# FFT filter and squared-ReLU FFN: a quarter of stage A moved, casts moved from VectorE to GpSimd

## The chip, the cores and the metric

The kernel runs on one core of a Trainium2 chip. Five engines work side by side: TensorE (PE, matmuls; its weight loads have a row of their own, PEld), VectorE (DVE), ScalarE (ACT), GpSimd (POOL) and SyncE (SP, which here issues nearly all DMAs). The metric is the device time of one execution in microseconds (us); lower is better.

## The reference

The input x has 8 batches of 3008 rows by 256 columns. Each batch is filtered along its rows in the frequency domain, and the result goes through a feed-forward network (FFN) with a squared ReLU.

```python
def _attn_ref(x, filt_r, filt_i):            # x (8, 3008, 256), filters (1505, 256)
    X = np.fft.rfft(x, axis=1)
    F = (filt_r + 1j * filt_i)[None, :, :]
    Y = X * F
    return np.fft.irfft(Y, n=x.shape[1], axis=1).astype(np.float32)

def _moe_ref(x, w_in, w_out):                # x (24064, 256), w_in (256, 2048), w_out (2048, 256)
    h = np.maximum(x @ w_in, 0.0)
    return (h * h @ w_out).astype(np.float32)
```

## The kernel before

The Fourier transform of 3008 = 64 x 47 points is done as matmuls with constant matrices, in stages, for one batch at a time:

- Stage A (`unit_a`, 16 units of a batch, four of them filling one tile u): matmuls into PSUM, and a cast of the 96x512 result into u in SBUF. In batches 2 to 7 the input is a tile of x cast to 16 bits (`cast_x`, 94x2048, four tiles a batch); batch 1 reads other tiles, `xw16`, and needs two matmuls a unit. Each full u is written to a DRAM buffer dU (`write_u`).
- `read_u` brings dU back in another layout as ut. Stage B (`unit_b`, 12 units) is two matmuls and, on DVE, the product with the filter, read from PSUM into prod, then two copies of half a tile across partitions (yf), then (`unit_s`) an add. `unit_p` takes yf through two more matmuls, ACT evacuates them into ze, and ze goes to DRAM (dZ).
- `read_z` brings dZ back as zt. Stage Y (`unit_y`, 16 units) is four small matmuls, evacuated by ACT (even units) or DVE (odd units) into yt, the FFN's input.

The FFN goes over 47 groups of 512 tokens. A group has eight slots. `ffn_g1` computes an eighth of the hidden layer, four matmuls into psH; ACT applies the ReLU into h; DVE squares h in place (`ffn_sq`); `ffn_g2` computes a half of one 128-token block of the group before (eight matmuls, psO). The loop at lines 728 to 739 writes the order out by hand: in slot s comes g1 of this group, the FFT work planned for place 0, g2 of the group before, the FFT work of place 1, the output, the square. Each engine works through its own instructions in that order, so an instruction that waits holds all behind it on its engine.

`fft_plan(b)` (line 610) says in which slot which unit of batch b runs. Slots are counted from a first slot of the batch: 0 for batch 1, and 40, 88, 136, 184, 232, 280 for batches 2 to 7, all multiples of eight. In batch 1 the plan also holds the rest of batch 0's stage Y and the four casts of W_out (`cast_wout`, 128x1024 each, on DVE). In batch 1 three quarters of stage A are done ahead of the loop by `chunk_a`; the plan has the last four units, 12 to 15, in slots 8 and 9. Stage B takes slots 14 to 31 in batch 1 and 19 to 37 later. The x of the next batch is loaded and cast in the same plan: two loads ahead of stage B's middle, and two that wait for the casts of the first two, since the pool of x in 32 bits has two buffers.

Tiles come from pools with a fixed number of buffers: a new tile waits until the last readers of the one that had its buffer are done. The ones that matter: psF (two buffers, shared by stages A, B, P and Y in turn), psH (two), `p_u` (u, three), `p_x16` (x in 16 bits, and `xw16`, four), `p_x32` (two), `p_h2` (h, and in the beginning W_out in 32 bits, two). In group 0 there is no g2 yet, so its slots are about half as long as the others.

Of the kernel before, what the change touches and what calls it, by code (L numbers as in the profile page):

```python
# [9 lines left out]
F16 = mybir.dt.float16  # L10
# [100 lines left out]
def kernel(  # L111
# [9 lines left out]
    nc = tc.nc  # L121
    B, S, D = x.shape
# [18 lines left out]
    p_x16 = ctx.enter_context(tc.tile_pool(name="p_x16", bufs=4))  # L141
    p_u = ctx.enter_context(tc.tile_pool(name="p_u", bufs=3))
# [14 lines left out]
    def psF(name):  # L157
        return pps.tile([128, 512], F32, tag="psF", name=name, bufs=2)
# [176 lines left out]

    x16s, us, uts, prods, zes, zts, yts = {}, {}, {}, {}, {}, {}, {}

    def cast_x(b, c, eng=nc.vector):
        t = p_x16.tile([94, 8, D], F16, tag="x16", name=f"x16_{b}_{c}")
        eng.tensor_copy(out=t, in_=x32s.pop((b, c))[0:94])  # L340
        x16s[(b, c)] = t

    def write_u(b, c):
        nc.sync.dma_start(
            out=dU[b].rearrange("(m q) d -> q m d", q=96)[:, 8 * c:8 * c + 8, :],
            in_=us.pop((b, c)))

    def unit_a(b, a):

        c, i = divmod(a, 4)  # L350
        if i == 0:
            us[(b, c)] = p_u.tile([96, 8, D], F16, tag="u", name=f"u_{b}_{c}")
        ps = psF(f"psA_{b}_{a}")
        m = slice(2 * i, 2 * i + 2)
        if b == 1:
            nc.tensor.matmul(ps[0:96, :], s1[:, c // 2, :], xw16[(b, 2 * (c % 2))][:, m, :],
                             start=True, stop=False)
            nc.tensor.matmul(ps[0:96, :], s1[0:120, 2 + c, :], xw16[(b, 1)][0:120, m, :],
                             start=False, stop=True)
        else:  # L360
            nc.tensor.matmul(ps[0:96, :], sSA, x16s[(b, c)][:, m, :], start=True, stop=True)  # L361
        o = us[(b, c)][:, 2 * i:2 * i + 2, :]
        pv = ps[0:96, :].rearrange("p (a d) -> p a d", d=D)
        if a % 2 == 0:
            nc.scalar.copy(out=o, in_=pv)  # L365
        else:
            nc.vector.tensor_copy(out=o, in_=pv)  # L367
        if i == 3:
            write_u(b, c)
# [240 lines left out]
    def fft_plan(b):  # L610

        plan = {}

        def put(r, place, f, *a):
            plan.setdefault((r, place), []).append((f, a))

        if b == 1:
            for n in range(4, 16):
                put(n if n < 8 else n + 2 if n < 12 else 2 * n - 7, n % 2, unit_y, 0, n)
            for k in range(4):  # L620
                put((4, 5, 7, 7)[k], 1, cast_wout, k, nc.vector)
        t0 = 2 if b == 1 else 6
        for a in range(12 if b == 1 else 0, 16):
            put(t0 + a // 2, a % 2, unit_a, b, a)
        put(10 if b == 1 else 14, 1, read_u, b)
        t0 = 14 if b == 1 else 19
        for p in range(12):
            r = t0 + (17 if b == 1 else 18) * p // 11
            put(r, 0, unit_b, b, p)
            put(r, 0, unit_s, b, p)  # L630
            put(r + 2, 1, unit_p, b, p)
        t0 = 34 if b == 1 else 40
        for c in range(4):
            put(t0, 1, read_z, b, c)
        if b + 1 < B:
            for c in range(2):
                put(t0 - 13, 1, load_x, b + 1, c)
            for c in range(4):
                r = t0 - 8 + 3 * c
                put(r, 1, cast_x, b + 1, c)  # L640
                if c < 2:
                    put(r, 1, load_x, b + 1, c + 2)
        for n in range(16):
            put((38 if b == 1 else 45) + n // 2, n % 2, unit_y, b, n)
        return plan
# [14 lines left out]
    for k in range(2):  # L660
        c = slice(12 * k, 12 * k + 12)
# [26 lines left out]
    for k in range(6):  # L688
        if k % 3 == 0:
            sSPx.append(p_u.tile([128, 12, 128], F16, tag="u", name=f"sSPx_{k}"))  # L690
        c, o = slice(4 * k, 4 * k + 4), slice(4 * k % 12, 4 * k % 12 + 4)
# [31 lines left out]
    for b in range(1, B):  # L723
        first = (b * S // TG) * SLOTS - (48 if b > 1 else 40)
        for (r, place), w in fft_plan(b).items():
            work[(first + r, place)] = w

    for s in range((NG + 1) * SLOTS):
        g, k = divmod(s, SLOTS)
# [40 lines left out]
```

## Time and profile before

| | us |
|---|---|
| median of 3 runs | 793.43 |
| lowest, highest | 793.39, 793.74 |
| the profiled execution | 793.69 |
| its span, first to last instruction | 791.9 |

| line, engine, what | count | mean ns | busy us |
|---|---|---|---|
| L566 ACT, ReLU into h | 376 | 1024 | 384.9 |
| L570 DVE, square of h | 376 | 685 | 252.6 |
| L453 DVE, product from PSUM (batches 1 to 7) | 84 | 1218 | 102.3 |
| L460 and L461 DVE, copies into yf | 168 | 289 and 288 | 48.5 |
| L467 DVE, add into yf | 84 | 425 | 35.7 |
| L340 DVE, cast of x, 94x2048 | 24 | 1216 | 29.2 |
| L333 DVE, cast of W_out, 128x1024 | 4 | 683 | 2.6 |
| L365 ACT, L367 DVE, evacuation of u | 50, 50 | 572, 687 | 28.6, 34.3 |
| L222 POOL, cast of xw, 128x1024 | 5 | 1138 | 5.5 |

"Busy" adds up the durations of a group. PE's rows overlap, so a busy PE says that a matmul was in flight, not that it ran at its peak; how far one start lies behind the last says more. GpSimd's last instruction begins at 35.15 us as part of a row of four that takes 3.99 us; after that it is idle to the end. The granted TensorE clock is 1.00 throughout.

### The profile page before, as it was taken

What the parts mean: (1) busy time and instruction counts of PE and PEld (TensorE: products, weight loads), DVE (VectorE), ACT (ScalarE), POOL (GpSimd) and SP (SyncE); (2) the same over time, 40 slices, a digit from 0 to 9 for tenths busy, and PEclk for the clock granted to TensorE, in tenths of its full rate; (3) what the DMA queues carried; (4) which work ended last, traced back from release to release, by engine and by line L of the source; (5) the groups of instructions that cost most, each with busy time, mean ns of one, the idle gap of its engine ahead of it and who ended that gap; (6) DMA issues with size and microseconds to landing.
All of it is one profiled execution on the core that took longest, in us unless ns stands there. A gap on an engine that the chain in (4) does not pass through costs nothing.

```text
span 791.9 us, 14822 instructions
## 1 busy us (share of the span) xinstructions
PE 778.9 (98%) x6102; PEld 552.5 (70%) x6102; DVE 550.3 (69%) x897; ACT 557.4 (70%) x711; POOL 23.6 (3%) x36
## 2 busy tenths in 40 slices
PE   8989999999999999999999999999999999999998
PEld 5746667667676777867777676776767677676666
DVE  6866994579755897559965699556995579553342
ACT  3976776777777777767776777676777777776664
POOL 3800000000000000000000000000000000000000
PEclk9999999999999999999999999999999999999999
DMA  9994554346814557154562555424563332611111
GB/s 363 368 260 153 146 157 111 93 135 167 205 42 112 167 155 180 48 173 135 132 167 65 163 147 155 112 80 148 159 180 86 97 133 66 147 40 41 41 41 54
DMA packets 88571, 107.32 MB, mean 136 GB/s; under 512 B 6336, under 2 KB 79040, under 8 KB 84288
## 3 DMA queue, kind: packets, MB, share of 16 engines
q1 hardware_dynamic: 88296, 106.19, 46.5%
q8 instruction: 48, 0.79, 0.4%
q10 hardware_dynamic: 144, 0.18, 0.1%
q14 instruction: 19, 0.16, 0.1%
q0 software_dynamic: 64, 0.00, 0.0%
HBM read 58.12 MB, written 48.23 MB: 134 GB/s over the span
## 4 chain that ended last, share of the span: by engine, by line
PE 89%; DVE 6%; DMA 3%; ACT 1%; SPq 0%; issue 0%; DVEq 0%; ACTq 0%
PE psO L579 40%; PE psH L562 38%; PE psA L361 3%; PE psY L532 2%; PE psB L445 2%; DMA f<-in_filt_i_dram 2%; PE psP L496 2%; DVE prod L453 2%; DVE h L570 1%; DMA wout<-in_moe_w_out_dram 1%; PE psf L287 1%; PE psf L290 1%; DVE yf L467 0%; ACT sF L298 0%; DVE yf L461 0%; ACT h L566 0%
## 5 line engine op out<-in xcount | busy, mean ns | idle before, releaser
L566 ACT ACTIVATE h<-psH 128x1024 f16<-128x1024 f32 x376 | 384.9, 1024 | 189.3 <-PE psH L562 186.7
L579 PE MATMUL psO<-sWout,h 128*128 128x256 f16 x3008 | 388.9, 272 | 0.6 <-DVE h L570 0.6
L562 PE MATMUL psH<-yt,sWin 128*128 128x512 f16 (+7 forms) x1728 | 386.9, 351 | 1.6 <-DVE yt L541 0.7
L579 PEld LDWEIGHTS <-h 128*128 128x128 f16 x3008 | 290.6, 98 | 79.1 <-DVE h L570 0.9
L570 DVE TENSOR_TENSOR h<-h 128x1024 f16<-128x1024 f16 x376 | 252.6, 685 | 104.7 <-ACT h L566 104.5
L562 PEld LDWEIGHTS <-sWin 128*128 128x128 f16 x1728 | 159.5, 98 | 101.7 <-issue 3.3
L453 DVE TENSOR_TENSOR prod<-psB,sF 128x1024 f16<-128x1024 f32 x84 | 102.3, 1218 | 2.8 <-PE psB L445 2.8
L541 DVE CAST yt<-psY 128x376 f16<-128x376 f32 x62 | 34.0, 549 | 59.4 <-PE psY L532 59.4
L367 DVE CAST u<-psA 96x512 f16<-96x512 f32 x50 | 34.3, 687 | 47.3 <-PE psA L361 45.1
L498 ACT CAST ze<-psP 128x512 f16<-128x512 f32 x84 | 49.1, 585 | 17.2 <-PE psP L496 14.7
L590 ACT COPY ost<-psO 128x512 f32<-128x512 f32 (+1 forms) x96 | 55.8, 581 | 6.8 <-PE psO L579 5.3
L532 PE MATMUL psY<-sC,zt 112*128 112x94 f16 x512 | 42.4, 205 | 1.4 <-DMA zt<-dZ 1.4
L532 PEld LDWEIGHTS <-zt 112*128 112x128 f16 x512 | 35.1, 98 | 11.6 <-issue 1.6
L467 DVE TENSOR_TENSOR yf<-prod,yf 128x512 f16<-128x512 f16 x84 | 35.7, 425 | 2.9
L361 PE MATMUL psA<-x,sC 94*96 94x512 f16 x96 | 36.6, 382 | 0.0
L445 PE MATMUL psB<-ut,sSB 128*128 128x256 f16 x192 | 36.5, 273 | 0.0
L496 PE MATMUL psP<-yf,sSP 128*128 128x256 f16 x168 | 32.1, 272 | 0.5 <-DVE prod L453 0.3
L539 ACT CAST yt<-psY 128x376 f16<-128x376 f32 x66 | 30.9, 468 | 2.0 <-issue 1.7
L445 PEld LDWEIGHTS <-sSB 128*128 128x128 f16 x192 | 18.5, 98 | 19.5
L340 DVE CAST x<-x 94x2048 f16<-94x2048 f32 x24 | 29.2, 1216 | 0.0
L365 ACT CAST u<-psA 96x512 f16<-96x512 f32 x50 | 28.6, 572 | 0.0
L460 DVE COPY yf<-prod 64x512 f16<-64x512 f16 x84 | 24.3, 289 | 2.9
(65 smaller groups left out, 253.2 us busy)
## 6 DMA issues: line engine op xcount, KB each, us to landing
x<-in_x_dram SPq DMA_DIRECT2D x20, 768.0 KB
zt<-dZ SPq DMA_DIRECT2D x64, 192.0 KB
dU<-u SPq DMA_DIRECT2D x28, 384.0 KB
dZ<-ze SPq DMA_DIRECT2D x28, 384.0 KB
out_dram<-ost SPq DMA_DIRECT2D x66, 128.0 KB
out_dram<-ost SPq DMA_DIRECT2D x31, 256.0 KB
ut<-dU SPq DMA_DIRECT2D x7, 1024.0 KB
xw<-in_x_dram SPq DMA_DIRECT2D x6, 1024.0 KB
```

The costliest lines, as they stand in the source:

```text
L361: nc.tensor.matmul(ps[0:96, :], sSA, x16s[(b, c)][:, m, :], start=True, stop=True)
L445: nc.tensor.matmul(ps[:, i * D:(i + 1) * D], sSB[:, 2 * p + i, :], uts[b][:, 2 * p + i, :], start=True, stop=True)
L453: nc.vector.tensor_mul(out=prod, in0=ps.rearrange("p (a d) -> p a d", d=D).unsqueeze(1).to_broadcast([128, 2, 2, D]), in1=sF[:, :, 2 * p:2 ...
L467: nc.vector.tensor_add(out=yf, in0=prod[:, 0], in1=yf)
L496: nc.tensor.matmul(ps[:, i * D:(i + 1) * D], sSP[:, 2 * p + i, :], yf[:, i, :], start=True, stop=True)
L498: nc.scalar.copy(out=zes[(b, c)][:, 2 * i6:2 * i6 + 2, :], in_=ps.rearrange("p (a d) -> p a d", d=D))
L532: nc.tensor.matmul(ps[:, 94 * jj:94 * jj + 94], zt[:, 4 * (g % 2) + jj, dt * 128:(dt + 1) * 128], sSY, start=True, stop=True)
L562: nc.tensor.matmul(ps[:, i, o:o + n], sWin[:, dt, jt * 128:(jt + 1) * 128], yts[b][:, dt, r:r + n], start=(dt == 0), stop=(dt == 1))
L566: nc.scalar.activation(out=h2[:, 2 * s:2 * s + 2, :], in_=ps, func=AF.Relu)
L570: nc.vector.tensor_mul(out=v, in0=v, in1=v)
L579: nc.tensor.matmul(pso[g][:, t % 2, :], h2s[g][:, jt, t * 128:(t + 1) * 128], sWout[:, jt, :], start=(jt == 0), stop=(jt == NJT - 1))
L590: nc.scalar.copy(out=ost[:, h0:h0 + step, :], in_=pso[g][:, h0:h0 + step, :])
```

## The change

- `cast_x` runs on GpSimd instead of DVE, for all 24 casts (batches 2 to 7), and is planned one slot earlier. The loads of x tiles 2 and 3 are planned one slot later than before, two after the cast.
- `cast_wout` runs on GpSimd, planned in slots 1, 2, 4 and 5 instead of 4, 5, 7 and 7.
- Units 12 to 15 of batch 1's stage A are planned in slots 1 to 4, in group 0, instead of 8 and 9. Their u takes a buffer of `p_x16` instead of `p_u`, and DVE evacuates all four; ACT did two of them. Batches 2 to 7 keep ACT for even units.
- Units 8 to 11 of batch 0's stage Y are planned in slots 8 to 11 instead of 10 to 13. The others stay.

```diff
-    def cast_x(b, c, eng=nc.vector):
+    def cast_x(b, c, eng=nc.gpsimd):
...
         if i == 0:
-            us[(b, c)] = p_u.tile([96, 8, D], F16, tag="u", name=f"u_{b}_{c}")
+            pool, tag = (p_x16, "x16") if b == 1 else (p_u, "u")
+            us[(b, c)] = pool.tile([96, 8, D], F16, tag=tag, name=f"u_{b}_{c}")
...
-        if a % 2 == 0:
+        if a % 2 == 0 and b > 1:
             nc.scalar.copy(out=o, in_=pv)
         else:
             nc.vector.tensor_copy(out=o, in_=pv)
...
             for n in range(4, 16):
-                put(n if n < 8 else n + 2 if n < 12 else 2 * n - 7, n % 2, unit_y, 0, n)
+                put(n if n < 12 else 2 * n - 7, n % 2, unit_y, 0, n)
             for k in range(4):
-                put((4, 5, 7, 7)[k], 1, cast_wout, k, nc.vector)
-        t0 = 2 if b == 1 else 6
+                put((1, 2, 4, 5)[k], 1, cast_wout, k, nc.gpsimd)
+        t0 = 6
         for a in range(12 if b == 1 else 0, 16):
-            put(t0 + a // 2, a % 2, unit_a, b, a)
+            put(a - 11 if b == 1 else t0 + a // 2, a % 2, unit_a, b, a)
...
             for c in range(4):
-                r = t0 - 8 + 3 * c
+                r = t0 - 9 + 3 * c
                 put(r, 1, cast_x, b + 1, c)
                 if c < 2:
-                    put(r, 1, load_x, b + 1, c + 2)
+                    put(r + 2, 1, load_x, b + 1, c + 2)
```

## The prediction

> **What bounds the kernel now.** I read the busy shares first, then the chain that ended last, the busy time by stage, and the timeline where the stages differ.
>
> ```profile
> PE 778.9 (98%) x6102; PEld 552.5 (70%) x6102; DVE 550.3 (69%) x897; ACT 557.4 (70%) x711; POOL 23.6 (3%) x36
> PE 89%; DVE 6%; DMA 3%; ACT 1%; SPq 0%; issue 0%; DVEq 0%; ACTq 0%
> ...
> 48.00:61.00 13.00, 11.29 (x78) 5.81 (x79) 9.11 (x16) 9.36 (x13) 0.00 (x0) 1.00 1.09 313
> 73.00:94.00 21.00, 20.51 (x160) 14.64 (x159) 20.40 (x37) 15.61 (x21) 0.00 (x0) 1.00 0.48 139
> 127.00:200.00 73.00, 73.00 (x572) 51.17 (x571) 53.62 (x92) 52.88 (x69) 0.00 (x0) 1.00 0.42 122
> ```
>
> The first line says TensorE (PE) is nearly always occupied. The chain gives it 89% and VectorE (DVE) 6%; all but a sliver of DVE's links lie between 55 and 114 us. In the table (stretch, length, then busy PE, weight load, DVE, ACT, POOL, clock, DMA share) PE has gaps in 48-61 and 73-94, and none in 127-200: from batch 2 on DVE costs nothing today, though it is itself full while it works on a batch's stage B. So little can be won, and a full DVE can lose its cover in five batches.
>
> How much can be won: a slot (one step of the loop) without FFT work takes 1.74 us (starts of psO at 65.79 and 67.53). From the spacing of PE's rows in the timeline a unit_a of batch 1 adds 0.43, unit_b 0.22, unit_p 0.22, unit_y 0.17. Group 0's slots do half a slot (0.87). From 49.71 to the first psO at 60.84, nine halves, four unit_y and one unit_a make 8.9 us; 11.1 were taken: 2.2 lost. In slots 14 to 33 the same sum falls short of the rows by 0.38, 0.43 and 0.76: 1.6 lost. No change of this kind can win more than 3.8 us, which is 0.5%.
>
> ```profile
> 57.44 0.60 DVE sWout L333
> 58.04 1.20 DVE h L570 x2
> 59.24 0.47 DVE yt L541
> ...
> 11.61 0.69 DVE L222 CAST xw<-xw 128x1024 f16<-128x1024 f32 x1 [1.20 <-DMA xw<-in_x_dram]
> 20.56 1.51 DVE L222 CAST f<-f 128x1024 f16<-128x1024 f32 x1 [0.26 <-DMA f<-in_filt_i_dram]
> 11.64 1.56 POOL L222 CAST xw<-xw 128x1024 f16<-128x1024 f32 x1 [8.98 <-DMA xw<-in_x_dram]
> 20.49 1.04 POOL L222 CAST f<-f 128x1024 f16<-128x1024 f32 x1 [2.37 <-DMA f<-in_filt_i_dram]
> ```
>
> The first three (chain) are group 0's loss: the W_out cast stands ahead of the squares and of the yt cast that slot 8 needs. The last four (timeline) are the same cast four times. Alone it is 0.69 on DVE and about 1.0 on POOL (four in 3.99 us at 35.15). Where both engines cast at once, the one that began 0.03 or 0.07 us later took 1.56 or 1.51: it stood still while the other ran.
>
> [...] the twelve products of batch 0 (L453, 24 to 40 us) ran beside POOL at a mean 1.217, against 1.218 for those without it. For the square (L570) and the add (L467), two SBUF inputs each, this trace has no case. [...]
>
> **The change part by part.**
>
> 1. *Price of a moved x cast.* POOL casts of 512 and 1504 columns take 0.607 and 1.440 us: 0.84 ns a column, so 2048 columns are 0.607 + 1536 x 0.00084 = 1.90 us (an estimate; DVE paid 1.216). For 1.9 us copies, adds and squares may not start on DVE; a product may. The product is 1.22 long, so one cast holds DVE between 0.7 (POOL starts with a product) and 1.9 (it starts before anything else). Nothing stands in POOL's queue, so it starts when x lands, not at its slot; casts 0 and 1 come almost together, some 5 slots ahead of their old place. Loads 2 and 3 no longer wait on SP behind a DVE cast; their move by two slots costs nothing.
>
> 2. *Batches 2 to 6 (a stage B each, casting for the next batch).* All five stand alike against the groups, for their first slots are multiples of 8. Worked for batch 2: the two x loads go out at 177.97; DMA share is about 1 until 186 and 0.00 in 187-188, so I take the landings as 184.2 (half the bytes) and 187.0.
> Cast 0 asks at 184.2, inside the square that began at 184.19, and gets the lock at 184.8, with the product of 184.79. That ends at 186.01; the next copy waits to 186.7: 0.7 late. Cast 1 asks at 187.0, among copy, copy, add, and gets in at 187.3: the add is held to 189.2 and ends at 189.6 instead of 187.08.
>
> ```profile
> 186.34 0.29 DVE L461 COPY yf<-prod 64x512 f16<-64x512 f16 x1
> 186.66 0.42 DVE L467 TENSOR_TENSOR yf<-prod,yf 128x512 f16<-128x512 f16 x1
> 187.01 1.29 DVE L570 TENSOR_TENSOR h<-h 128x1024 f16<-128x1024 f16 x2
> 188.21 1.22 DVE L453 TENSOR_TENSOR prod<-psB,sF 128x1024 f16<-128x1024 f32 x1
> 188.67 0.38 PE L496 MATMUL psP<-yf,sSP 128*128 128x256 f16 x2
> ```
>
> The last row is unit_p, which reads that add's yf. [...] it can start at about 189.65: PE stops for about 0.95 us, and group matmuls stand behind it in order. Afterwards PE is late too and DVE has lost three casts of 1.22 of its own, so I add nothing for casts 2 and 3. Sum: 5 x 0.95 = +4.75; ends 0 (every cast begins with a product) and 5 x 2 = 10 (every cast holds 1.9).
>
> 3. *Batch 1's stage B (slots 14 to 33).* Two of batch 2's x casts (101.49, 108.87) leave a DVE that is on the path, at most 2.4 gained. But cast 0 now lands at about 94.5 (DMA stays near 1 from 88 to 98, half the bytes by then) and holds the add and square there by 1.9; cast 1 at 98.2 falls into the next product, now 97.3 to 98.5, and holds the copies to 100.1. The add of that pair ends at 101.05 instead of 97.7. PE's unit_p at 99.94 waits for it, 1.3; the next unit_b needs the psF buffer that the product, now 102.25 to 103.5, frees: 1.2 more. The stall of 0.76 at 114.16 (late square behind a DVE cast) goes. Sum 1.3 + 1.2 - 0.76 = +1.75, ends -1.6 and +4.
>
> 4. *Group 0 (slots 0 to 9).* The four unit_a move from slots 8 and 9 to 1 to 4, their 1.74 us of PE into gaps; all four evacuations are now DVE's (0.687, two of them 0.572 on ACT before), and the four W_out casts (0.683) leave it. By the yt cast that slot 8 waits for, DVE owes seven squares, four u casts, two yt casts: 4.8 + 2.75 + 1.1 = 8.65 from 52.0, so 60.65 instead of 59.71. Slot 8's first half ends at 61.5 with four unit_a done; before, the same work stood done at 60.56 + 1.74 = 62.3: 0.8 gained. The W_out casts, 1.0 each on POOL, run when their data land (DMA is full from 47 to 61), among the squares; the u casts read PSUM and cover about 0.7 of each. I take 0.8 for what is left: sum 0, ends -2.2 and +1.5. The u buffer (from x16, its last readers in batch 0) adds no wait; the write of u and the read of ut go out some 7 us earlier, for a unit_b that waits for nothing now. unit_y 8 comes to slot 8, where its zt has just landed (ACT's wait at 60.98): within the ends.
>
> Sum: 4.75 + 1.75 + 0 = +6.5 on the profiled execution's 793.69 (span 791.9 and 1.8 around it), 800.2; the median of the runs is 0.26 below that execution, so 799.9, taken as 800.0.
>
> **The rivals.** *B: [...]* DVE's operations follow each other without a gap (two squares take 1.29, not 2 x 0.685), so POOL may get in only at a product or a pause. Then a cast costs DVE 0.7 to 1.2, no more than the one taken away: batches 2 to 6 stay at 0, batch 1 ends between -1 and +1, group 0 near 0: 793.5. For it: that overlap. Against it: POOL has asked first, and the row at 20.49 shows no yielding once it holds. *C, the other side: the square and the add do not collide with POOL.* No row shows that they do. Then only the copies, 0.58 of each 3.4 us, can be held, DVE has 1.22 less per cast, and group 0's 0.8 and most of batch 1's 1.6 come home: 793.4 - 0.8 - 1.4 = 791.2, at best 789.6. It decides if a square running across a POOL cast stays at 0.69. *D: POOL starts late or is slower* than 1.9, say 3: every hold grows by 1.1, two to three of four reaching PE: about 806.
>
> **How the numbers follow.** Forecast A 0.60, B 0.17, C 0.18, D 0.05. A measurement of this kernel tells 0.2% (1.6 us) from no change. A and D are slower; of B 0.13 is the same, 0.04 slower; of C 0.13 is faster, 0.05 the same; the tail of A at its low ends gives 0.02 to the same and 0.01 to faster. So faster 0.14, same 0.20, slower 0.66. A's own range is 795 to 804; the whole range runs from 791.0, just under C, to 804.
>
> **What would show it.** Right: in stage B of batches 2 to 6 rows of L461, L467 or L570 stretched to 1 to 2.5 us where POOL's L340 runs at about 1.9, and PE waits at L496 on DVE; 127-200 no longer full. Wrong: squares at 0.69 beside L340 (C); L340 always starting with L453 (B), or much over 1.9 long (D). Step 4 is wrong if the first psO comes before 60 or after 63 us.

## The result and the profile after

The changed kernel takes 804.99 us (median of 4 runs, 804.41 to 807.07); the kernel before took 793.59 in the same session. The ratio is 1.0145, 95% interval 1.0124 to 1.0166: 11.4 us slower, where 6.5 were forecast, and 1.0 us above the upper end of the stated range. The profiled execution took 804.41, its span 802.6, 10.7 more than before.

First the page of the changed kernel: busy time of the engines, the chain by engine, and five of its groups. (Lines of the code are one further down than before from `unit_a` on.)

```profile
PE 781.7 (97%) x6102; PEld 551.9 (69%) x6102; DVE 553.1 (69%) x871; ACT 556.7 (69%) x709; POOL 78.1 (10%) x64
PE 72%; DVE 25%; ACT 1%; DMA 1%; issue 1%; ACTq 0%; SPq 0%; DVEq 0%
...
L571 DVE TENSOR_TENSOR h<-h 128x1024 f16<-128x1024 f16 x376 | 270.8, 733 | 116.1 <-ACT h L567 114.4
L454 DVE TENSOR_TENSOR prod<-psB,sF 128x1024 f16<-128x1024 f32 x84 | 102.2, 1217 | 1.8 <-PE psB L446 1.6
L340 POOL CAST x<-x 94x2048 f16<-94x2048 f32 x24 | 49.2, 2048 | 491.7 <-DMA x<-in_x_dram 490.6
L468 DVE TENSOR_TENSOR yf<-prod,yf 128x512 f16<-128x512 f16 x84 | 42.1, 501 | 2.9
L461 DVE COPY yf<-prod 64x512 f16<-64x512 f16 x84 | 28.9, 344 | 2.9
```

DVE gave away 29.2 us of x casts and 2.6 of W_out casts, and is as busy as before: 553.1 against 550.3. A held instruction counts as busy (the add at 199.45 below stands as 1.99 us, against 0.42 for an add at 188.09). The squares grew by 18.2 us in all (270.8 against 252.6), the adds by 6.4, the first copies by 4.6, although their number and shapes are the same; the products, which read PSUM, did not grow (1217 ns against 1218). DVE's share of the chain went from 6% to 25%. (That share does not measure a loss: it is 22% in experiment 1 below, which costs 0.3%.)

What PE itself waited for, from the two pages (first two lines before, last two after; the last figures are PE's idle time there and what ended it):

```profile
L445 PE MATMUL psB<-ut,sSB 128*128 128x256 f16 x192 | 36.5, 273 | 0.0
L496 PE MATMUL psP<-yf,sSP 128*128 128x256 f16 x168 | 32.1, 272 | 0.5 <-DVE prod L453 0.3
...
L446 PE MATMUL psB<-ut,sSB 128*128 128x256 f16 x192 | 36.4, 272 | 6.4 <-DVE prod L454 6.4
L497 PE MATMUL psP<-yf,sSP 128*128 128x256 f16 x168 | 32.2, 273 | 2.5 <-DVE yf L468 2.0
```

Most of the new idle time stands at unit_b, which waits for a product (6.4 us), and less at unit_p, which waits for an add (2.0 us).

Next the busy time by stage, two stretches before and three of the changed kernel (stretch, length, busy PE, weight loads, DVE, ACT, POOL, then clock, DMA share and GB/s):

```profile
222.00:316.00 94.00, 94.00 (x728) 66.50 (x726) 69.48 (x116) 67.60 (x87) 0.00 (x0) 1.00 0.50 135
316.00:411.00 95.00, 95.00 (x739) 68.15 (x737) 69.89 (x116) 68.59 (x89) 0.00 (x0) 1.00 0.49 134
...
127.00:200.00 73.00, 71.73 (x559) 49.77 (x557) 53.82 (x89) 51.50 (x68) 4.90 (x3) 1.00 0.42 121
222.00:316.00 94.00, 92.07 (x706) 64.52 (x704) 70.21 (x110) 66.31 (x86) 8.06 (x4) 1.00 0.46 129
316.00:411.00 95.00, 93.33 (x724) 66.61 (x723) 70.10 (x111) 66.96 (x87) 7.89 (x4) 1.00 0.46 128
```

PE was full in all three before; now it has gaps in each, of 1.3 to 1.9 us. Where exactly, the starts of psO tell, slot by slot, from the timelines of both kernels. The shift is the start in the changed kernel less the start before; a step in it is time lost at that slot.

| part | steps of the shift, us | sum |
|---|---|---|
| start of the loop and group 0, to slot 14 | | -0.50 |
| batch 1's stage B | slot 27: 1.09, slot 34: 0.39 | 1.48 |
| batch 2 | slots 72, 73: 0.12, 1.25; slot 76: 0.49 | 1.86 |
| batch 3 | 119: 1.52; 121: 0.75; 125: 0.12 | 2.40 |
| batch 4 | 168, 169: 0.44, 1.25; 172: 0.49 | 2.17 |
| batch 5 | 216, 217: 0.13, 1.25; 221: 0.12 | 1.51 |
| batch 6 | 264, 265: 0.42, 1.25; 269: 0.12 | 1.80 |
| all | | 10.7 |

Steps under 0.1 us are left out. Here is batch 2's loss in the timeline of the changed kernel (start, length, engine, instruction; in brackets what ended an idle time):

```profile
185.61 2.00 POOL L340 CAST x<-x 94x2048 f16<-94x2048 f32 x1 [71.73 <-DMA x<-in_x_dram]
187.03 0.73 DVE L461 COPY yf<-prod 64x512 f16<-64x512 f16 x1
188.09 0.42 DVE L468 TENSOR_TENSOR yf<-prod,yf 128x512 f16<-128x512 f16 x1
188.23 2.03 POOL L340 CAST x<-x 94x2048 f16<-94x2048 f32 x1 [0.62 <-DMA x<-in_x_dram]
188.43 2.98 DVE L571 TENSOR_TENSOR h<-h 128x1024 f16<-128x1024 f16 x2
189.65 0.38 PE L497 MATMUL psP<-yf,sSP 128*128 128x256 f16 x2
191.33 1.21 DVE L454 TENSOR_TENSOR prod<-psB,sF 128x1024 f16<-128x1024 f32 x1
194.75 1.22 DVE L454 TENSOR_TENSOR prod<-psB,sF 128x1024 f16<-128x1024 f32 x1
196.02 0.38 PE L446 MATMUL psB<-ut,sSB 128*128 128x256 f16 x2 [1.08 <-DVE prod L454]
199.13 2.03 POOL L340 CAST x<-x 94x2048 f16<-94x2048 f32 x1 [8.87 <-DMA x<-in_x_dram]
199.45 1.99 DVE L468 TENSOR_TENSOR yf<-prod,yf 128x512 f16<-128x512 f16 x1
201.50 0.39 PE L497 MATMUL psP<-yf,sSP 128*128 128x256 f16 x2 [0.32 <-DVE yf L468]
```

Cast 0, at 185.61, makes the copy of 187.03 0.44 us late. Cast 1 asks at 188.23, while the add runs; its 2.03 us, less the 1.89 of a cast that waits for nothing, put its true start at about 188.4, where the add ends. The two squares behind it take 2.98 us instead of 1.29. The product that followed them at 188.21 before comes at 191.33, 2.1 us late after allowing for the 1.0 us by which everything here is late. unit_p at 189.65 does not notice, for its add was through. The delay stays on DVE, which has no gap over 0.04 us here, and surfaces at the unit_b of slot 73 (196.02): it needs a psF buffer that the product of 194.75 still reads. Cast 2 then holds an add, and the unit_p of slot 75 waits for that.

### The profile page after: what moved, and what is told of

It reads as the page before. It is cut to its first block, busy times and chain, and to the rows that moved or that the text cites. A ratio compares the mean times of both kernels' runs of the same rounds, so it can differ in the third digit from the quotient of the medians.

```text
span 802.6 us, 14856 instructions
## 1 busy us (share of the span) xinstructions
PE 781.7 (97%) x6102; PEld 551.9 (69%) x6102; DVE 553.1 (69%) x871; ACT 556.7 (69%) x709; POOL 78.1 (10%) x64
## 4 chain that ended last, share of the span: by engine, by line
PE 72%; DVE 25%; ACT 1%; DMA 1%; issue 1%; ACTq 0%; SPq 0%; DVEq 0%
PE psO L580 31%; PE psH L563 30%; DVE prod L454 8%; DVE h L571 7%; DVE yf L468 4%; PE psA L362 3%; PE psY L533 2%; DVE yf L461 2%; DVE yf L462 2%; PE psB L446 1%; PE warm L268 1%; PE psP L497 1%; DMA wout<-in_moe_w_out_dram 1%; PE psf L287 1%; PE psf L290 1%
## 5 line engine op out<-in xcount | busy, mean ns | idle before, releaser
L571 DVE TENSOR_TENSOR h<-h 128x1024 f16<-128x1024 f16 x376 | 270.8, 733 | 116.1 <-ACT h L567 114.4
L454 DVE TENSOR_TENSOR prod<-psB,sF 128x1024 f16<-128x1024 f32 x84 | 102.2, 1217 | 1.8 <-PE psB L446 1.6
L340 POOL CAST x<-x 94x2048 f16<-94x2048 f32 x24 | 49.2, 2048 | 491.7 <-DMA x<-in_x_dram 490.6
L499 ACT CAST ze<-psP 128x512 f16<-128x512 f32 x84 | 49.2, 585 | 21.5 <-PE psP L497 19.1
L468 DVE TENSOR_TENSOR yf<-prod,yf 128x512 f16<-128x512 f16 x84 | 42.1, 501 | 2.9
L461 DVE COPY yf<-prod 64x512 f16<-64x512 f16 x84 | 28.9, 344 | 2.9
```

The costliest lines, as they stand in the source:

```text
L454: nc.vector.tensor_mul(out=prod, in0=ps.rearrange("p (a d) -> p a d", d=D).unsqueeze(1).to_broadcast([128, 2, 2, D]), in1=sF[:, :, 2 * p:2 ...
L468: nc.vector.tensor_add(out=yf, in0=prod[:, 0], in1=yf)
L499: nc.scalar.copy(out=zes[(b, c)][:, 2 * i6:2 * i6 + 2, :], in_=ps.rearrange("p (a d) -> p a d", d=D))
L571: nc.vector.tensor_mul(out=v, in0=v, in1=v)
```

## The experiments

Three theories are set against each other. Theory L (lock): a GpSimd cast keeps DVE's copies, adds and squares from starting, and a full DVE hands that on to PE. Rival S (schedule): the moved loads, units and buffers cost by themselves. Rival T (late x): the slower cast delivers x late.

**1. The x casts back on DVE, all else as changed.**

```diff
-    def cast_x(b, c, eng=nc.gpsimd):
+    def cast_x(b, c, eng=nc.vector):
```

> The changed kernel with the x casts back on VectorE, everything else of the change kept (slots, loads, W_out on GpSimd, u in an x16 buffer). Lock theory (GpSimd's x casts hold VectorE's copies, adds and squares): the 9.7 us of batches 2 to 6 and most of batch 1's 1.5 us are gone, group 0's gain of about 0.5 us stays: 792 to 794 us. Schedule theory (the moved loads and units cost by themselves): 803 us or more.

Measured: 796.55 us, ratio to the kernel before 1.0032 (1.0019 to 1.0046). About 8.4 of the 11.4 us go, as L says, but it stays 2.6 us above the upper end expected. Batch 1's stage B is still 0.7 longer than before, and each of batches 2 to 6 still loses 0.38 at its slot 73 or the like. The cast is planned one slot earlier than before, and on DVE, which takes it in its planned place, that is enough to make one product late. A piece of S is true, then, for casts on DVE: 5 x 0.38. In the changed kernel a cast begins when x has landed, whatever its slot, so this piece can't simply be taken off its loss. The 0.5 us that group 0 was to keep are not there either: up to slot 14 this kernel is 0.30 behind the kernel before.

**2. The kernel before with only the x casts on GpSimd.**

```diff
-    def cast_x(b, c, eng=nc.vector):
+    def cast_x(b, c, eng=nc.gpsimd):
```

> The kernel before with nothing changed but the engine of the 24 x casts, GpSimd for VectorE. Lock theory: most of the loss comes with this one word, 802 to 806 us, with squares, copies and adds of up to 2.4 us beside a GpSimd cast. Schedule theory: 793.5 us, as before.

Measured: 808.14 us, ratio 1.0179 (1.0164 to 1.0194), 2.1 us above the upper end expected. This one word costs at least as much as the whole change (the two intervals just overlap); its span is 12.3 longer, 12.0 of it in batches 2 to 6, and the steps at slots 73, 169, 217 and 265 are the same 1.25. S falls as the main cause.

**3. The casts still on GpSimd, but behind stage B.** On the changed kernel:

```diff
-                put(t0 - 13, 1, load_x, b + 1, c)
+                put(t0 - 4, 1, load_x, b + 1, c)
...
-                r = t0 - 9 + 3 * c
-                put(r, 1, cast_x, b + 1, c)
+                put(t0 + 1 if c < 2 else t0 + 6, 1, cast_x, b + 1, c)
...
-                    put(r + 2, 1, load_x, b + 1, c + 2)
+                    put(t0 + 2, 1, load_x, b + 1, c + 2)
```

> The changed kernel with the casts still on GpSimd, but the x loads planned behind stage B, so that the casts run where VectorE has gaps. Lock theory: VectorE rows are still held beside a cast, but TensorE does not wait for them: 791 to 793.5 us. If a late x is what costs (the cast takes 2.05 us in place of 1.22), this makes x later still: 805 us or more. Schedule theory: 803 us or more.

Measured: 793.50 us, ratio 0.9993 (0.9985 to 1.0001). The same engine casts the same tiles (1.89 us in the median), the first loads of x are planned nine slots later, and the loss is gone. T falls. The one step left after batch 1, 0.54 at slot 85, is a unit_y that waits for its zt: two x loads are issued at 200.70, ahead of zt's from 208.88. With the x loads one slot earlier (experiment 9) the step is not there.

**4. Every cast done twice.** On the changed kernel:

```diff
-        eng.tensor_copy(out=t, in_=x32s.pop((b, c))[0:94])
+        x32 = x32s.pop((b, c))
+        eng.tensor_copy(out=t, in_=x32[0:94])
+        eng.tensor_copy(out=t, in_=x32[0:94])
```

> The changed kernel with every x cast done twice on GpSimd, one behind the other, so 4.1 us instead of 2.05 a tile. Lock theory: each of the five batches loses at least as much again, 815 to 830 us, and the waits stay with TensorE behind VectorE's products and adds. Schedule theory: 805 us, since GpSimd has nothing else to do. Late x: 805 to 807 us, since stage A comes many slots later.

Measured: 839.37 us, ratio 1.0566 (1.0548 to 1.0584). The direction is L's, the size is not: it is 9 us above the upper end expected, and the span grew by 45.5 us, four times the 10.7 of single casts. A part of that has another cause. In this profile the granted TensorE clock is at half for 30.7 us in all, in seven stretches of 3.4 or 6.8 us. Two stretches of 3 us, both with PE busy throughout, show what that means (third figure: busy PE with its matmuls; third from the end: the clock):

```profile
106.00:109.00 3.00, 3.00 (x12) 1.53 (x11) 2.95 (x4) 0.59 (x1) 2.24 (x2) 0.50 0.00 0
112.00:115.00 3.00, 3.00 (x24) 2.10 (x22) 2.92 (x6) 2.25 (x3) 0.00 (x0) 1.00 0.92 246
```

At half clock PE starts half as many matmuls here, 12 against 24. Each of the seven begins during a stop of PE of 1.97 to 2.95 us or within 1.3 us after it, so the half clock comes with the long stops; one stop of 1.98 us had no such stretch behind it. The stretches cost 15.4 us at most (an estimate: half of 30.7). At least 30 us, about three times the loss of single casts, are left for the second cast itself. Why that is more than twice is not shown. The changed kernel has full clock throughout its profile, and its longest stop in these stages is 1.34 us.

**5. Every cast cut into eight of 256 columns.**

```diff
+        for i in range(8):
+            eng.tensor_copy(out=t[:, i:i + 1, :], in_=x32[0:94, i:i + 1, :])
```

> The changed kernel with each GpSimd x cast split into eight of 256 columns (0.4 us each, about 3.1 us a tile in place of 2.05). If the length of one hold is what matters (VectorE slips in between the pieces and no row is held over about 0.5 us), TensorE's stops shrink: 795 to 800 us. If the total time under the lock matters (each piece again goes ahead of a waiting VectorE row), the loss stays or grows: 804 to 810 us.

Measured: 795.06 us, ratio 1.0020 (1.0014 to 1.0027). From this kernel's groups and timeline:

```profile
L342 POOL CAST x<-x 94x256 f16<-94x256 f32 x192 | 92.7, 529 | 440.9 <-DMA x<-in_x_dram 414.0 <-PE psH L565 23.1 <-DVE prod L456 3.8
...
184.66 7.64 POOL L342 CAST x<-x 94x256 f16<-94x256 f32 x16 [68.04 <-DMA x<-in_x_dram]
186.00 0.29 DVE L463 COPY yf<-prod 64x512 f16<-64x512 f16 x1
186.31 0.39 DVE L464 COPY yf<-prod 64x512 f16<-64x512 f16 x1
186.73 0.50 DVE L470 TENSOR_TENSOR yf<-prod,yf 128x512 f16<-128x512 f16 x1
187.15 1.68 DVE L573 TENSOR_TENSOR h<-h 128x1024 f16<-128x1024 f16 x2
```

GpSimd is busy almost twice as long with x, 92.7 us against 49.2 (its own waits included; a piece takes 0.39 at least, so a tile 3.1 in place of 1.89), and the five batches lose 2.6 us in place of 9.7. The rows alternate: sixteen pieces last 7.64 us, and beside them a copy takes 0.39 (0.29 at 186.00), two squares 1.68 (1.29 before). So the length of one hold decides, more than their sum.

**6 and 7. Half of the casts each.** On the changed kernel, casts 0 and 1 on DVE and 2 and 3 on GpSimd, and the mirror:

```diff
-                put(r, 1, cast_x, b + 1, c)
+                put(r, 1, cast_x, b + 1, c, nc.vector if c < 2 else nc.gpsimd)
```

> The changed kernel with x casts 0 and 1 back on VectorE and casts 2 and 3 on GpSimd. Lock theory: the 1.25 us stop at slot 73 of batch 2 and its like in the other batches shrinks to the 0.38 us that the earlier VectorE casts leave in the run with all x casts on VectorE; the stop of about 0.5 us behind cast 2 stays: 797 to 800 us. If any GpSimd work costs the same wherever it falls: 801 us, half the loss.

> The mirror: x casts 0 and 1 on GpSimd, 2 and 3 on VectorE. Lock theory: the stop near slot 73 stays, 1.25 to 1.5 us a batch, the one behind cast 2 goes or is small: 800 to 803 us, more than the mirror run.

Measured: 808.70 us, ratio 1.0184 (1.0163 to 1.0205), for the first, and 802.22, 1.0113 (1.0096 to 1.0130), for the mirror. The mirror came as expected, with its 1.25 at slots 73, 121, 169 and 217. The first was expected to be mild and is no better than the changed kernel. (Its four executions run from 805.06 to 809.79, and the profiled one is the slowest; it holds one stretch of 3.4 us at half clock, from 117.8 us, behind a stop of 2.12.) Its timeline in batch 3 shows what the expectation left out:

```profile
299.94 1.90 POOL L340 CAST x<-x 94x2048 f16<-94x2048 f32 x1 [84.40 <-PE psB L446]
299.99 2.93 DVE L340 CAST x<-x 94x2048 f16<-94x2048 f32 x1
303.44 1.21 DVE L454 TENSOR_TENSOR prod<-psB,sF 128x1024 f16<-128x1024 f32 x1
305.78 0.38 PE L497 MATMUL psP<-yf,sSP 128*128 128x256 f16 x2 [1.09 <-DVE yf L468]
308.38 1.89 POOL L340 CAST x<-x 94x2048 f16<-94x2048 f32 x1 [6.54 <-DMA x<-in_x_dram]
308.40 2.01 DVE L462 COPY yf<-prod 64x512 f16<-64x512 f16 x1
```

GpSimd's cast began 0.05 before DVE's own, so DVE paid for both: 2.93 us for a cast of 1.22. That half the GpSimd work costs half the loss is wrong. It matters which row is caught, and how full DVE is just then.

**8. The kernel before with only the W_out casts on GpSimd** (slots 1, 2, 4 and 5, as in the change).

> The kernel before with nothing changed but the four W_out casts, on GpSimd in slots 1, 2, 4 and 5. From the first psH to the psO of slot 14 the kernel before takes 23.76 us and the changed one 23.3 to 24.3. If the W_out casts on VectorE are what holds group 0, this takes 22.7 to 23.3 there and 792.5 to 793.3 us in all; if the holds of the GpSimd casts eat that, 23.8 there and 793.6 us in all.

Measured: 793.93 us, ratio 1.0007 (0.9999 to 1.0016). From the first psH to the psO of slot 14 it takes 24.4 us, against 23.76 before: no gain. A row of two squares (57.19 us) takes 2.29 us beside a pair of W_out casts; such a row took 1.28 before. In the changed kernel that stretch took 23.7, and in the runs that keep its group 0 (those of 1 and 3 to 7) 23.3 to 24.6. Four kernels with the old group 0 (before, 2, and the next two) took 23.76 each.

**9 and 10. The kernel before with x loaded and cast behind stage B**, on GpSimd and on DVE: loads 0 and 1 at `t0 - 5`, casts at `t0 + 1` and `t0 + 8`, loads 2 and 3 at `t0 + 3`.

> The kernel before with the x casts on GpSimd and the x loads planned behind stage B (loads one slot earlier than in the first run with late casts, so that stage Y does not wait for its zt); W_out and stage A as before. Lock theory: batches 2 to 6 lose nothing and batch 1's late square at slot 33 is no longer late, so 0.7 to 1.2 us are won: 792.2 to 793 us. If holds still reach TensorE: 793.5 to 796 us.

> The same late loads and casts, with the casts on VectorE. If the engine does not matter once the casts are out of stage B, this gives the same 792.2 to 793 us as the casts on GpSimd; if GpSimd is worth having there, this is 1 us or more slower than the run on GpSimd.

Measured: 792.59 us, ratio 0.9990 (0.9983 to 0.9997), on GpSimd, the only kernel here whose interval lies below the kernel before, by 0.1%; and 804.47, ratio 1.0132 (1.0114 to 1.0149), on DVE. In the first the only step over 0.1 us is -0.76 at slot 34, batch 1's late square; PE is full from batch 2 on, though squares are still held (the single one at 207.88 takes 1.43 us, where the median is 0.685), as its timeline shows:

```profile
203.29 3.72 DVE L570 TENSOR_TENSOR h<-h 128x1024 f16<-128x1024 f16 x3
203.97 1.89 POOL L340 CAST x<-x 94x2048 f16<-94x2048 f32 x1 [68.37 <-DMA x<-in_x_dram]
205.42 0.38 PE L496 MATMUL psP<-yf,sSP 128*128 128x256 f16 x2
206.68 2.08 POOL L340 CAST x<-x 94x2048 f16<-94x2048 f32 x1 [0.82 <-PE psH L562]
207.88 1.43 DVE L570 TENSOR_TENSOR h<-h 128x1024 f16<-128x1024 f16 x1 [0.87 <-ACT h L566]
```

The run on DVE was to be 1 us or more slower if GpSimd is worth having there; it is 12 us slower, and for a cause other than a hold, in its timeline:

```profile
224.88 1.22 DVE L340 CAST x<-x 94x2048 f16<-94x2048 f32 x1 [2.00 <-DMA x<-in_x_dram]
226.94 1.22 DVE L340 CAST x<-x 94x2048 f16<-94x2048 f32 x1 [0.84 <-DMA x<-in_x_dram]
228.08 0.54 DVE L541 CAST yt<-psY 128x376 f16<-128x376 f32 x1
228.68 0.33 PE L532 MATMUL psY<-sC,zt 112*128 112x94 f16 x4 [1.35 <-DVE yt L541]
```

DVE's cast waits for its data, and the yt cast behind it, and PE behind that, wait too. (Its profiled execution is 12.0 us longer than the kernel before; 5.1 of them fall at slots 282 and 283, at one such stop of 2.90 us with 3.4 us of half clock behind it.) On GpSimd nothing stood behind the waiting cast. The pair of runs thus shows which engine can afford to wait in this plan; it does not test holds.

## Why the prediction fell short

That a GpSimd cast holds DVE's rows, and that a full DVE hands this on to PE, was right. The trace of before shows a hold only between two casts; that copies, adds and squares are held the same way was not shown until the changed kernel ran. Where the held time reaches PE in batches 2 to 6, and so how much, was not. By its steps:

- *Step 1, the price.* Right in the main. An x cast that waits for nothing takes 1.89 us (1.90 forecast); the mean of 2.05 holds GpSimd's own waits. It starts when x lands. Holds of 0.7 to 1.9 were forecast; a copy of 0.73 (0.44 too long, less than forecast), an add of 1.99 (1.6 too long) and a pair of squares 1.7 too long stand above.
- *Step 2, batches 2 to 6: the step that failed.* It put down 0.95 us a batch, at unit_p behind a held add, and "nothing for casts 2 and 3". Measured: 9.74 us for the five, 1.95 each in place of 0.95. The working followed DVE's order up to the first row of PE that reads yf, and stopped there. Cast 1 came one row later than taken, on the squares; unit_p was not late at all, and the held time went on down a DVE without idle time to the next product and so to psF, where unit_b stopped: 1.25 us at slot 73 and at its like in batches 4 to 6, by itself more than the 0.95; in batch 3 1.52 and 0.75. Nor did the saving of DVE's own casts cancel cast 2, as the step assumed: in batches 2 and 4 another 0.49 follows at slots 76 and 172. The mirror run, with casts 2 and 3 on DVE, still loses 1.4 us in three of the five batches, 2.5 and 0.2 in the others. The step's upper end, 10, held the truth; the range for the total was drawn at 804 all the same, too low for it.
- *Step 3, batch 1.* +1.75 forecast, +1.48 measured, and that near only by luck, for two of its three terms were wrong. Right is the stop of unit_b at psF, 1.09 us where 1.2 were forecast: here the working did follow the delay to the buffer. But unit_p, at 99.45, did not stop (1.3 forecast), since cast 1 came at 96.94 and held the add then, not the copies of the next product. And the stop of 0.76 at the late square, which was to go, stayed and grew by 0.39: cast 3 held a copy for it.

```profile
97.23 1.99 DVE L468 TENSOR_TENSOR yf<-prod,yf 128x512 f16<-128x512 f16 x1
99.45 0.38 PE L497 MATMUL psP<-yf,sSP 128*128 128x256 f16 x2
101.62 0.38 PE L446 MATMUL psB<-ut,sSB 128*128 128x256 f16 x2 [0.93 <-DVE prod L454]
111.99 1.89 POOL L340 CAST x<-x 94x2048 f16<-94x2048 f32 x1 [6.99 <-DMA x<-in_x_dram]
112.00 2.02 DVE L462 COPY yf<-prod 64x512 f16<-64x512 f16 x1
115.14 0.39 PE L580 MATMUL psO<-sWout,h 128*128 128x256 f16 x2 [0.98 <-DVE h L571]
```

- *Step 4, group 0.* 0 forecast. The stretch from the first psH to slot 14 took 23.69 in place of 23.76, and 24.15 in the mean of the seven kernels that have this group 0; experiment 8 shows that the GpSimd holds eat what W_out's leaving DVE gives. The other 0.4 of the -0.50 is where the loop began (first psH at 49.28 instead of 49.71).
- *The rivals.* B, that GpSimd gets in only at a product or a pause of DVE: refuted, its cast got in at about 188.4 between an add and a square that followed without a gap. C, that squares and adds do not collide: refuted by the rows above; the longest single square went from 0.69 us to 2.38, the longest add from 0.43 to 2.13. Rows of DVE that read PSUM did not grow: each of the 84 products takes 1.225 at most in both kernels, each cast into u from the loop's stage A 0.687, before and after. D, a slower cast: refuted, 1.89. One reading for B and C was a little off: eleven of the twelve products of batch 0 ran beside GpSimd, not all twelve.

The sum: 4.75 + 1.75 + 0 = 6.5 forecast; 9.74 + 1.48 - 0.50 = 10.7 on the two profiled executions.

## What to carry to other kernels

Work moved from VectorE to GpSimd was not off VectorE here: while a GpSimd cast ran, VectorE's copies, adds and squares stood still (an add took 1.99 us in place of 0.42, two squares 2.98 in place of 1.29); the products, which read PSUM, did not (1.217 against 1.218 in the mean). Two remedies worked in this kernel: to move the casts to where VectorE has gaps (792.59 us against 808.14 with the casts in stage B), and to cut each into short pieces (795.06 against 804.99). When a wait enters a full in-order engine, follow it until that engine next idles, past the first reader that escapes; the bill may come some slots later, at a buffer (here 1.25 us at a unit_b that starts 7.8 us after the cast asked). And casts that had to wait for a late x cost 12 us more on VectorE, where other work stood behind them, than on GpSimd, where none did (804.47 against 792.59).

## What was not expected

- Two casts in place of one cost four times as much (45.5 against 10.7 us of span), at most 15.4 of it by the clock, and half of the casts no less than all of them (808.70 against 804.99, intervals that just overlap): the loss is far from proportional to GpSimd's time.
- Long stops of PE had half clock behind them: nine stretches in three profiles (experiments 4, 6 and 10), all begun during a stop of 1.97 to 2.95 us or within 1.3 us after it. (Three more stand near 49 us, where the loop starts, behind stops of about 1 us.)
- Cutting a cast in eight made GpSimd 1.9 times as busy and took three quarters of the five batches' loss away (2.6 against 9.7 us).
- One slot earlier costs 0.38 us a batch for a cast on DVE, in a stage whose rows show no idle PE before.
- The loop's start differs by up to 0.5 us between kernels with the same code ahead of it (first psH at 49.20 to 49.73, one profiled execution each), as much as the -0.50 up to slot 14.
